# Decay tables read as 2 KB rows, and weight tiles loaded among the first attention loads

## The chip, the cores and the metric

The kernel runs on one core of one Trainium2 chip. The metric is the device time of one execution in microseconds (us). The kernel before took 637.29 us, the median of three runs (636.66 to 637.46).

## What is computed

A decayed linear attention (2 batches, 8 heads, 768 positions, head size 64), whose output is reshaped to 1536 tokens by 512 features, goes through two feed-forward blocks. The reference computes the attention block by block:

```python
Dmask = np.where(rel >= 0, lam[:, None, None] ** rel[None, :, :], 0.0)
lam_pow = lam[:, None, None] ** (pos[None, :, None] + 1)
intra = np.einsum('bhic,bhjc->bhij', qb, kb) * Dmask[None]
intra = np.einsum('bhij,bhjd->bhid', intra, vb)
inter = np.einsum('bhid,bhde->bhie', qb * lam_pow[None], kv_state)
out[:, :, sl] = intra + inter
kb_dec = kb * rev_pow[None]
kv_state = lam_block[...] * kv_state + np.einsum('bhsd,bhse->bhde', kb_dec, vb)
```

Then `h = x @ w_in`, an activation (0 below -1, `(h + 1)**2 / 4` up to 1, `h` above), `x = g @ w_out` with 2048 hidden features; then `(x @ w_a * x @ w_b) @ w_out` with 1536. The weights arrive as float64 bits.

## The kernel before, in words

**Attention.** The 1536 tokens are 12 chunks of 128, six for each batch. `load_chunk` (L122) brings four tiles of a chunk, 256 KB each: qT, kT, kn and vn, issued on SP's queue. For a chunk `att_scores` (L128) makes 8 score products on TensorE into two PSUM banks; `att_mask` (L141) multiplies the keys by the decay (kd, L145, on VectorE for chunk 0, else on GpSimd), the scores by the decay mask (pm, L154, VectorE) and the queries by the powers (qd, L162, GpSimd, for chunk 3 VectorE); `att_state` (L166) makes the new state from kd and vn; `att_out` (L188) adds the two output products and splits the result into the high and low parts of `xy` (L211 ScalarE, L212 VectorE).

**Tables.** The masks come from powers of lam. `powers` (L77) loads lam, raises it on GpSimd (L90), and a zero row is written to a scratch tensor `rows` in DRAM; `store_powers` (L100) writes the powers there; `tables` (L103) reads them back with shifted, overlapping access patterns into `dmask` (512 KB) and `tabq` (256 KB), in runs of 128 floats (512 B). All of these but the zero row's store go through SP's queue.

**Weights.** `load_w` (L227) loads a [128, 512] weight tile of float64 bits (512 KB); `split_w` (L236) turns it into two float32r parts: two operations on ScalarE (L252, L256), four on VectorE (L253, L257, L260, L263), the rounding on ScalarE (L284) and the remainder on GpSimd (L285). Each `split_w` ends with the next `load_w`. Four raw buffers are there.

**Feed-forward.** `h_bank` (L289) and `ab_bank` make the inner products, 12 matmuls of 512 columns each (L273), `y_bank` and `o_bank` the outer ones. The stages run over groups of hidden features and three blocks of 512 tokens. The attention of chunks 4 to 11 is put between the first inner products by `att_step` (L389).

**Order.** SP's and TensorE's instructions stay in the order of the program; VectorE, ScalarE and GpSimd are ordered by a scheduler. Each engine works its own instructions in order. The order around the change stands in L347 to L382: powers, the first loads, `store_powers`, `tables`, more loads, 10 products of zeros (`warm`, L94), the scores of chunks 0 to 2, 4 products of zeros, then the attention of chunks 0 to 3 with one `split_w` after the state of chunk 2 and one at its end; `ahead(4)` (L438) brings the splits to four before the first stage. A tile pool `t2` of 12 buffers holds the temporaries of masks and splits, `acc` of 16 holds the loaded chunks.

## Time and profile before

| | before |
|---|---|
| median of three runs | 637.29 us |
| span of the profiled execution | 635.7 us |
| TensorE matmul busy | 615.7 us (97%) |
| VectorE busy | 380.9 us (60%) |
| ScalarE busy | 247.4 us (39%) |
| GpSimd busy | 253.0 us (40%) |
| mean granted TensorE clock | 0.987 |

The profile covers one execution. Its span, from the first to the last instruction, is 1.6 us below the median of the runs; no other time of that execution is shown. Engines in the rows: PE is TensorE, PEld its weight loads, DVE VectorE, ACT ScalarE, POOL GpSimd, SP SyncE; a q after the name means the engine's queue of instructions that issue DMAs and wait. L145 is line 145 of the kernel. "idle before <-releaser" tells how long an engine stood idle before an instruction and what ended that. PEclk is the granted TensorE clock as a share of full speed.

### The profile page before, as it was taken

The numbers are of one execution on the slowest core, as the hardware profiler recorded it, in microseconds if no ns is written. First come the engines' busy times: TensorE is split into PE (matmuls) and PEld (weight loads), VectorE is DVE, ScalarE is ACT, GpSimd is POOL, SyncE is SP. The second block draws the span as 40 slices with busy tenths as digits, with TensorE's granted clock in tenths as the row PEclk, the third lists the DMA queues.
The fourth block names the chain that finished last, engine by engine and source line by source line (L and its number), as shares of the span: only waits on it lengthen the run. The fifth ranks groups of instructions, "written<-read, shape, count | busy, mean of one in ns | idle before, by whom it ended". The sixth has DMA issues, their size and how long they took to land.

```text
span 635.7 us, 7943 instructions
## 1 busy us (share of the span) xinstructions
PE 615.7 (97%) x3012; PEld 507.3 (80%) x3012; DVE 380.9 (60%) x568; ACT 247.4 (39%) x421; POOL 253.0 (40%) x207
## 2 busy tenths in 40 slices
PE   5898799999999999999999999999999999999998
PEld 2777588888888888888888888888888888888886
DVE  0799794746976797588764433455545555555323
ACT  0245243454543354435643544433333333333110
POOL 2657763433533444354665432222223333333210
PEclk9789799999999999999999999999999999999999
DMA  6968321111210121021102122111111111210013
GB/s 185 379 243 293 111 68 34 66 35 66 100 66 34 66 84 56 34 94 66 67 34 67 67 67 67 66 65 62 56 51 69 64 68 66 67 34 1 1 67 133
DMA packets 20503, 52.70 MB, mean 83 GB/s; under 512 B 2408, under 2 KB 4208, under 8 KB 20464
## 3 DMA queue, kind: packets, MB, share of 16 engines
q1 hardware_dynamic: 20448, 52.18, 23.8%
q8 instruction: 24, 0.39, 0.3%
q14 instruction: 15, 0.12, 0.1%
q10 hardware_dynamic: 16, 0.00, 0.0%
HBM read 49.02 MB, written 3.15 MB: 82 GB/s over the span
## 4 chain that ended last, share of the span: by engine, by line
PE 89%; DVE 4%; DMA 2%; POOL 2%; issue 1%; ACT 1%; SPq 0%; DVEq 0%; POOLq 0%; ACTq 0%
PE ps L273 86%; PE ps L199 1%; PE ps L195 1%; PE ps L174 1%; DMA dmask<-rows 1%; DVE v L263 1%; DVE v L260 1%; DMA lamp<-in_lam 1%; DVE hc L253 1%; DVE v L257 1%; DVE pm L154 0%; DMA rows<-base 0%; POOL qd L162 0%; POOL kd L145 0%; DVE x L212 0%
## 5 line engine op out<-in xcount | busy, mean ns | idle before, releaser
L273 PE MATMUL ps<-y,win 128*128 128x512 f32 x864 | 198.8, 389 | 0.0
L273 PEld LDWEIGHTS ps<-y,win 128*128 128x128 f32 x864 | 162.2, 188 | 33.7
L273 PE MATMUL ps<-x,win 128*128 128x512 f32 x576 | 137.1, 396 | 3.3 <-DVE pm L154 2.6
L273 PE MATMUL ps<-g,wout 128*128 128x512 f32 x576 | 132.6, 389 | 0.0
L273 PEld LDWEIGHTS ps<-x,win 128*128 128x128 f32 x576 | 109.0, 190 | 27.4 <-ACT x L211 2.8
L273 PEld LDWEIGHTS ps<-g,wout 128*128 128x128 f32 x576 | 108.0, 188 | 22.6 <-issue 0.2
L285 POOL TENSOR_TENSOR win<-v,win 128x512 fp32r<-128x512 f32 x40 | 52.2, 1304 | 151.7 <-ACT win L284 151.7
L285 POOL TENSOR_TENSOR g<-r,g 128x512 fp32r<-128x512 f32 x48 | 67.2, 1399 | 85.3 <-ACT g L284 59.8
L273 PE MATMUL ps<-wout,g 128*128 128x512 f32 (+1 forms) x438 | 100.8, 386 | 0.0
L253 DVE TENSOR_SCALAR hc<-hc 128x512 f32<-128x512 f32 x68 | 37.2, 548 | 101.7 <-ACT hc L252 101.4
L273 PEld LDWEIGHTS ps<-wout,g 128*128 128x128 f32 x438 | 81.5, 188 | 16.7
L317 DVE TENSOR_TENSOR acc<-acc,ps 128x512 f32<-128x512 f32 (+1 forms) x97 | 64.7, 678 | 47.2 <-PE ps L273 47.2
L285 POOL TENSOR_TENSOR wout<-v,wout 128x512 fp32r<-128x512 f32 x28 | 36.8, 1313 | 85.1 <-ACT wout L284 85.0
L260 DVE SCALAR_TENSOR_TENSOR v<-raw,v 128x512 int32<-128x512 int32 x68 | 67.4, 991 | 2.3
L293 DVE SCALAR_TENSOR_TENSOR r<-r 128x512 f32<-128x512 f32 x48 | 37.9, 789 | 50.1 <-ACT r L292 50.1
L263 DVE CUSTOM_DVE_ANT_0 v<-v,c 128x1024 uint16<-128x1024 uint16 x68 | 56.3, 828 | 6.0
L284 ACT CAST win<-v 128x512 fp32r<-128x512 f32 x40 | 24.9, 622 | 87.1 <-DVE v L263 87.1
L302 ACT COPY a<-ps 128x512 f32<-128x512 f32 x36 | 21.1, 587 | 95.0 <-PE ps L273 93.6
L285 POOL TENSOR_TENSOR g<-a,g 128x512 fp32r<-128x512 f32 x36 | 46.5, 1292 | 25.8 <-ACT g L284 25.8
L292 ACT ACTIVATE r<-ps,half 128x512 f32<-128x512 f32 x48 | 32.8, 683 | 46.9 <-PE ps L273 46.9
L257 DVE TENSOR_SCALAR v<-hc 128x512 int32<-128x512 int32 x68 | 43.9, 646 | 5.0 <-DVE hc L253 0.9
L252 ACT ACTIVATE hc<-raw 128x512 f32<-128x512 f32 x68 | 45.3, 666 | 0.9 <-DMA raw<-in_w1i 0.9
(46 smaller groups left out, 395.4 us busy)
## 6 DMA issues: line engine op xcount, KB each, us to landing
raw<-in_w2ab SPq DMA_DIRECT2D x24, 512.0 KB, 3.2
raw<-in_w1i SPq DMA_DIRECT2D x16, 512.0 KB, 3.3
raw<-in_w1o SPq DMA_DIRECT2D x16, 512.0 KB, 3.2
raw<-in_w2o SPq DMA_DIRECT2D x12, 512.0 KB, 3.3
qT<-in_att SPq DMA_DIRECT2D x12, 256.0 KB, 4.7
kT<-in_att SPq DMA_DIRECT2D x12, 256.0 KB, 4.5
kn<-in_att SPq DMA_DIRECT2D x12, 256.0 KB, 5.2
vn<-in_att SPq DMA_DIRECT2D x12, 256.0 KB, 5.1
```

The costliest lines, as they stand in the source:

```text
L252: nc.scalar.activation(out=hc.bitcast(F32), in_=high.bitcast(F32), func=ACTF.Abs)
L253: nc.vector.tensor_scalar(out=hc.bitcast(F32), in0=hc.bitcast(F32), scalar1=HIGH_MIN, scalar2=HIGH_MAX, op0=ALU.max, op1=ALU.min)
L257: nc.vector.tensor_scalar(out=v, in0=hc, scalar1=3, scalar2=0x3FFFFFFF, op0=ALU.logical_shift_left, op1=ALU.bitwise_and)
L260: nc.vector.scalar_tensor_tensor(out=v, in0=high, scalar=-0x40000000, in1=v, op0=ALU.bitwise_and, op1=ALU.bitwise_or)
L263: nc.vector.tensor_tensor(out=v, in0=v, in1=c, op=ALU.add)
L273: nc.tensor.matmul(out=ps, lhsT=l[a], rhs=r[b], start=(i == 0 and j == 0), stop=(i == n - 1 and j == 2))
L284: nc.scalar.copy(hi, src)
L285: nc.gpsimd.tensor_tensor(out=lo, in0=src, in1=hi.bitcast(F32), op=ALU.subtract)
L292: nc.scalar.activation(out=r, in_=ps, func=ACTF.Relu, scale=0.5, bias=half)
L293: nc.vector.scalar_tensor_tensor(out=r, in0=r, scalar=1.0, in1=r, op0=ALU.min, op1=ALU.mult)
L302: nc.scalar.copy(a, pa)
L317: nc.vector.tensor_tensor(out=total, in0=total, in1=ps, op=ALU.add)
```

## The change

The scratch tensor `rows` becomes two rows, one for the even and one for the odd heads, with the four heads of one exponent side by side: 128 x 4 zeros, 4 ones, then the powers 1 to 128. lam is read to all partitions, so that the power is one GpSimd operation with no VectorE work on the base before it. The loads and stores of the tables go through ScalarE's queue. A table is read as rows of 512 floats (2 KB), four heads interleaved, and turned to head-major order by one copy each on VectorE, ScalarE and GpSimd. In the written order the four first weight tiles are loaded among the first attention loads, two `split_w` stand ahead of the tables, the others after the states of chunks 1 and 3, the fourth chunk's loads one step earlier, and 8 products of zeros follow the scores of each of the chunks 0 to 2 (24 in place of 4).

```diff
-PITCH = 272
+PITCH = (2 * CH + 1) * H // 2
...
-    lamp = const.tile([128, 1], F32, name="lamp")
-    base = const.tile([128, 8], F32, name="base")
-    exi = const.tile([128, 8], I32, name="exi")
-    exf = const.tile([128, 8], F32, name="exf")
-    zrow = const.tile([H, CH + 1], F32, name="zrow")
-    dmask = const.tile([128, H, CH], F32, name="dmask")
+    lamp = const.tile([128, H], F32, name="lamp")
+    base = const.tile([128, 2, H // 2], F32, name="base")
+    exi = const.tile([128, H], I32, name="exi")
+    exf = const.tile([128, H], F32, name="exf")
+    one = const.tile([2, H // 2], F32, name="one")
+    dmask = const.tile([128, 2, H // 2, CH], F32, name="dmask")
...
-    rows = dram.tile([H, PITCH], F32, name="rows")
+    rows = dram.tile([2, PITCH], F32, name="rows")
...
     def powers():
-        nc.sync.dma_start(out=lamp, in_=bass.AP(tensor=lam.tensor, offset=lam.offset, ap=[[1, H], [0, 16], [1, 1]]))
-        nc.gpsimd.iota(exi, pattern=[[1, 8]], base=0, channel_multiplier=8)
-        nc.vector.memset(base, 0.0)
-        nc.vector.memset(zrow[:, 0:CH], 0.0)
-        nc.vector.memset(zrow[:, CH:CH + 1], 1.0)
+        nc.scalar.dma_start(out=lamp, in_=bass.AP(tensor=lam.tensor, offset=lam.offset, ap=[[0, 128], [1, H]]))
+        nc.gpsimd.iota(exi, pattern=[[0, H]], base=1, channel_multiplier=1)
+        nc.vector.memset(idle, 0.0)
+        zrow = t2("zrow")
+        nc.vector.memset(zrow[0:2], 0.0)
+        nc.vector.memset(one, 1.0)
         nc.vector.memset(half, 0.5)
-        nc.scalar.dma_start(out=rows[:, 0:CH + 1], in_=zrow)
-        nc.vector.tensor_scalar(out=exi, in0=exi, scalar1=127, scalar2=None, op0=ALU.bitwise_and)
         nc.vector.tensor_copy(exf, exi)
-        nc.vector.tensor_scalar(out=exf, in0=exf, scalar1=1.0, scalar2=None, op0=ALU.add)
-        nc.vector.tensor_scalar(out=base, in0=base, scalar1=lamp, scalar2=None, op0=ALU.add)
-        nc.gpsimd.tensor_tensor(out=base, in0=base, in1=exf, op=ALU.pow)
+        nc.scalar.dma_start(out=rows[:, 0:CH * H // 2], in_=zrow[0:2])
+        nc.scalar.dma_start(out=rows[:, CH * H // 2:(CH + 1) * H // 2], in_=one)
+        nc.gpsimd.tensor_tensor(
+            out=base, in0=lamp.rearrange("p (a e) -> p e a", e=2), in1=exf.rearrange("p (a e) -> p e a", e=2),
+            op=ALU.pow,
+        )
+        nc.scalar.dma_start(out=raw_ap((CH + 1) * H // 2, [[H // 2, 128], [PITCH, 2], [1, H // 2]]), in_=base)
...
-    def store_powers():
-        nc.sync.dma_start(out=raw_ap(CH + 1, [[PITCH, H], [8, 16], [1, 8]]), in_=base)
-
     def tables():
-        for i in range(2):
-            nc.sync.dma_start(
-                out=dmask[:, 4 * i:4 * i + 4], in_=raw_ap(1 + 4 * i * PITCH, [[1, 128], [PITCH, H // 2], [1, CH]])
-            )
-        for e in range(2):
-            nc.sync.dma_start(
-                out=tabq[64 * e:64 * e + 64],
-                in_=raw_ap(CH + 1 + e * PITCH, [[0, 64], [2 * PITCH, H // 2], [1, CH]]),
-            )
+        win = [t2("pw") for _ in range(3)]
+        for e in range(2):
+            nc.scalar.dma_start(out=win[e], in_=raw_ap(e * PITCH + H // 2, [[H // 2, 128], [1, 512]]))
+        for e in range(2):
+            nc.scalar.dma_start(
+                out=win[2][64 * e:64 * e + 64], in_=raw_ap(e * PITCH + (CH + 1) * H // 2, [[0, 64], [1, 512]])
+            )
+        turned = [w.rearrange("p (i a) -> p a i", a=H // 2) for w in win]
+        nc.vector.tensor_copy(dmask[:, 0], turned[0])
+        nc.scalar.copy(dmask[:, 1], turned[1])
+        nc.gpsimd.tensor_copy(tabq, turned[2])
...
-                in1=dmask[:, :, CH - 1:CH].rearrange("p (a e) i -> p a e i", e=2).to_broadcast([128, H // 2, 2, D]),
+                in1=dmask[:, :, :, CH - 1:CH].rearrange("p e a i -> p a e i").to_broadcast([128, H // 2, 2, D]),
...
-                in1=dmask.rearrange("p (a e) i -> p e a i", e=2)[:, i], op=ALU.mult,
+                in1=dmask[:, i], op=ALU.mult,
...
         powers()
-        nc.vector.memset(idle, 0.0)
         load_chunk(0, (0, 1))
+        load_w()
+        load_w()
+        load_chunk(0, (2, 3))
         load_chunk(1, (0, 1))
+        load_w()
+        load_chunk(1, (2, 3))
         load_chunk(2, (0, 1))
-        store_powers()
-        load_chunk(0, (2, 3))
-        tables()
-        load_chunk(1, (2, 3))
-        load_chunk(3, (0, 1))
+        load_w()
         load_chunk(2, (2, 3))
-        load_w()
-        load_chunk(3, (2, 3))
-        load_w()
+        load_chunk(3)
         warm(10)
         for c in range(3):
             att_scores(c)
-        warm(4)
+            warm(8)
+        split_w()
+        split_w()
+        tables()
         att_mask(0)
         att_state(0)
         att_mask(1)
         att_out(0)
         att_state(1)
         att_scores(3)
+        split_w()
         att_mask(2)
         att_out(1)
         att_state(2)
-        split_w()
         att_mask(3)
         att_out(2)
+        load_chunk(4)
         att_state(3)
-        load_chunk(4)
+        split_w()
         att_out(3)
-        split_w()
         load_chunk(5)
```

## Rows read from the trace of the kernel before

**Rows 1.** Busy time by stretches: us, busy (instructions) by engine, PEclk, DMA share, GB/s.
```profile
0.00:17.20 17.20, 8.81 (x62) 4.67 (x63) 1.92 (x11) 1.28 (x1) 3.38 (x9) 0.96 0.69 188
17.20:24.00 6.80, 6.78 (x49) 6.00 (x49) 4.13 (x9) 1.82 (x3) 4.02 (x5) 0.61 1.05 395
24.00:37.20 13.20, 11.29 (x107) 9.64 (x105) 12.18 (x20) 3.53 (x6) 10.50 (x12) 0.87 0.77 294
37.20:47.50 10.30, 10.30 (x78) 8.27 (x78) 10.17 (x16) 4.68 (x9) 3.52 (x3) 1.00 0.83 287
47.50:78.40 30.90, 24.98 (x196) 20.14 (x194) 26.81 (x39) 12.02 (x23) 23.71 (x22) 0.89 0.61 210
78.40:160.00 81.60, 80.87 (x442) 67.12 (x442) 54.06 (x73) 39.02 (x69) 33.42 (x26) 1.00 0.16 52
160.00:635.70 475.70, 472.66 (x2091) 391.42 (x2090) 271.62 (x405) 185.05 (x315) 174.51 (x133) 1.00 0.18 61
```

**Rows 2.** The timeline of PE: start us, us, operation, idle before and releaser.
```profile
6.48 1.16 PE L133 MATMUL ps<-qT,kT 64*128 64x128 f32 x16 [0.75 <-DMA kT<-in_att]
...
10.24 1.04 PE L98 MATMUL ps<-idle 128*128 128x512 bf16 x4
17.22 2.05 PE L174 MATMUL ps<-vn,kd 128*128 128x128 f32 x8 [5.94 <-DVE kd L145]
19.20 1.98 PE L199 MATMUL ps<-pm,vn 128*64 128x128 f32 x16
21.11 1.84 PE L174 MATMUL ps<-vn,kd 128*128 128x128 f32 x8
...
25.06 1.09 PE L199 MATMUL ps<-pm,vn 128*64 128x128 f32 x16
26.08 1.16 PE L174 MATMUL ps<-vn,kd 128*128 128x128 f32 x8
...
32.42 1.76 PE L195 MATMUL ps<-qd,st 128*128 128x128 f32 x8 [1.70 <-DVE qd L162]
34.11 1.98 PE L199 MATMUL ps<-pm,vn 128*64 128x128 f32 x16
...
71.42 0.80 PE L273 MATMUL ps<-x,win 128*128 128x512 f32 x1 [2.58 <-DVE pm L154]
```

**Rows 3.** The chain that ended last, 0 to 20 us: start us, us, what.
```profile
0.73 4.04 DMA lamp<-in_lam
...
5.68 1.65 POOL base L90
...
7.35 2.82 DMA rows<-base
...
10.62 5.69 DMA dmask<-rows
```

**Rows 4.** The timeline of DVE: first and last operation of the first split.
```profile
25.76 0.51 DVE L253 TENSOR_SCALAR hc<-hc 128x512 f32<-128x512 f32 x1
...
31.09 0.68 DVE L263 CUSTOM_DVE_ANT_0 v<-v,c 128x1024 uint16<-128x1024 uint16 x1
```

**Rows 5.** Groups of DVE by line, 17 to 80 us: busy us, mean ns.
```profile
L260 DVE SCALAR_TENSOR_TENSOR v<-raw,v 128x512 int32<-128x512 int32 x7 | 7.9, 1135 | 0.2
L257 DVE TENSOR_SCALAR v<-hc 128x512 int32<-128x512 int32 x7 | 6.5, 922 | 0.2
L253 DVE TENSOR_SCALAR hc<-hc 128x512 f32<-128x512 f32 x8 | 5.6, 698 | 0.2
L263 DVE CUSTOM_DVE_ANT_0 v<-v,c 128x1024 uint16<-128x1024 uint16 x7 | 5.4, 777 | 0.2
```

**Rows 6.** Groups by line of ACT and of POOL, 16 to 80 us.
```profile
L211 ACT CAST x<-ps 128x512 fp32r<-128x512 f32 x9 | 5.2, 578 | 26.7 <-PE ps L199 26.6
...
L162 POOL TENSOR_TENSOR qd<-qT,tabq 128x512 f32<-128x512 f32 x7 | 9.1, 1300 | 0.1
```

**Rows 7.** Waits of SP's queue, 0 to 60 us: total us, times, longest.
```profile
SPq L126 <- DMA dmask<-rows: 1.3, 1, 1.3
```

## The prediction

> **What bounds the kernel now.** I read the busy time by stretches first, because an average over the span hides where TensorE loses time. From 160 us to the end PE is busy 472.66 of 475.70 us at full clock, and from 78.4 to 160 us 80.87 of 81.60 [rows 1]. There the change touches nothing, and whatever it wins must be won before 78.4 us: PE then arrives at the saturated part earlier by that much, and the end moves with it.
>
> Before 78.4 us three stretches lose. Up to 17.2 us PE waits for the decay tables. From 17.2 to 37.2 us, the attention of chunks 0 to 3, PE is nearly always busy at first, but at a granted clock of 0.61, a mix of its two levels (1.2 and 2.4 GHz), and then 1.91 us idle (13.20 less 11.29) at 0.87. From 47.5 to 78.4 us it is idle 5.92 us, and the clock is 0.89 [rows 1]. In these stretches VectorE is the fullest engine: 12.18 of 13.20 us, 10.17 of 10.30, 26.81 of 30.90 [rows 1].
>
> The timeline of PE then says who ends the waits: 5.94 us before the first state product, for kd on VectorE; 1.70 us before chunk 3's output, for a qd on VectorE; 2.58 us at 71.42 us, for a mask product on VectorE [rows 2]. The chain of waits traces the first of them back: lam loaded 4.04 us, power 1.65, its store 2.82, the mask read back 5.69 [rows 3]. So the start hangs on a chain of DMAs, and the rest up to 78.4 us on VectorE, which does the weight splits between the masks: the first one's four operations begin at 25.76 us, and the last of them at 31.09 us runs just ahead of the qd that PE waits for [rows 2, 4]. A split there costs VectorE 1.135 + 0.922 + 0.698 + 0.777 = 3.53 us [rows 5]. Meanwhile VectorE works 1.92 us in the first 17.2 us [rows 1].
>
> **The change, part by part. The table chain.** The power no longer waits for VectorE's four small operations between lam's arrival at 4.77 us and 5.68 us; it can start 0.9 us earlier, if lam lands as before. Its store moves to ScalarE's queue and now meets the loads issued by SP. The nearest rows for a small store are 2.82 us, with few loads beside it, and 5.69 us for a read among others [rows 3]; I take 3.7, nearer the first since it moves as few bytes, so the gain of 0.9 is spent. The tables' bytes are the same, 0.79 MB, in 384 pieces of 2 KB where there were 1536 of 512 B. Their time lies between 2.0 us (0.79 MB at the 395 GB/s of the saturated stretch [rows 1]) and a full wait behind SP's loads (the first rival). I take what the read took before, 5.69 us: larger pieces speak for less, loads of 6.29 MB beside it for more. So the mask lands at about 16.3 us, as before. New are the three turning copies. No row has a strided copy; the nearest are a ScalarE cast of 0.58 us and a GpSimd operation of 1.30 us of the same size [rows 6]. I take 0.7 us on the path (VectorE and ScalarE run side by side), bounds 0.6 and 1.3. The copy on GpSimd feeds only qd and the state, which come later; uncovered it would cost 1.3 us. kd then starts near 17.1 us.
>
> **The zeros and the clock.** PE must do the scores of chunk 2 and 8 zeros before the first state product. Up to the end of chunk 2's queries and keys SP's queue now has 4.19 MB: three weight tiles of 0.52 MB, chunks 0 and 1 whole (1.05 MB each) and these 0.52 MB. Chunk 0's tiles (0.52 MB) let the scores start at 6.48 us [rows 2]; without lam ahead of them on SP I take 5.5. The other 3.67 MB at 395 GB/s are 9.3 us, and about 0.6 MB of the tables in between 1.6 us: 16.4 us. Scores of 1.16 us and eight zeros of 1.04 / 4 = 0.26 us [rows 2] give 16.4 + 1.16 + 2.1 = 19.7 us for the first state product, 2.5 us after the 17.22 of before: **2.5 us lost**. The bounds are nothing (kd later than all this) and the late tables below. In return PE comes to it straight from work. Before, after 5.94 us idle, it did state, output, state in 2.05 + 1.98 + 1.84 us; the same groups later take 1.16, 1.09 and 1.16 [rows 2]: **2.5 us won**, or nothing if the zeros don't hold the clock.
>
> **Splits out of the attention.** Two splits, 7.1 us of VectorE, move into a time when it did 1.92 us in 17.2. ScalarE (1.28 us busy) and GpSimd (3.38 us) have room there too [rows 1]. Tiles three and four are loaded early as well, so that their splits can follow in the wait or between the masks; what that gives stands with the late stage. Gone is the 1.70 us wait before chunk 3's output and the slow clock behind it (1.76 + 1.98 against 1.16 + 1.09, 1.5 us) [rows 2]: **3.2 us won**; between 0 and 3.2 if another wait takes the place. Late next is GpSimd: it is busy 4.02 + 10.50 of the 20 us up to 37.2 [rows 1], none of that shrinks, and the turned table comes on top. I take **1 us lost** for it.
>
> **The stage of 47.5 to 78.4 us.** At most PE wins its idle 5.92 us and the clock, 0.11 of 24.98 = 2.7 us: 8.6 us. From 37.2 on VectorE had 10.17 + 26.81 = 37.0 us of work; less the third and fourth split, 7.1, which have moved ahead of it, it has 29.9, against PE's 10.30 + 24.98 - 2.7 = 32.6 [rows 1]. So PE becomes the longer of the two, but GpSimd (27.2 us in the same time) and short chains keep some waits. I take six tenths, **5.3 us won**; bounds 0 and 8.6.
>
> **Edits at no cost.** load_chunk(4) moves past one state product on SP's queue, where later weights already wait for buffers. The 16 zeros after chunks 0 and 1 run while PE would wait for data; without that wait they would cost 16 x 0.26 = 4.2 us. The masks' new layout leaves the operations' sizes alone; if they turned slow, 24 of them would each cost VectorE something, so I look at them.
>
> **Sum:** -2.5 + 2.5 + 3.2 - 1.0 + 5.3 = 7.5 us. The profiled span is 635.7 us, 1.6 us below the median of 637.29, which I take as what lies around it: 628.2 + 1.6 = **629.8 us**.
>
> **The rivals. First, the tables come late, and the gain is small.** The transfers share engines that the loads saturate: the DMA share is 1.05 at 395 GB/s as soon as weights and chunks are queued together [rows 1]. If the reads got through only behind all loads, 6.29 + 0.79 MB at 395 GB/s from about 4 us end at 22 us; with copy and kd the first state product is at 23.4 us, 6.2 us late. Of the terms above 2.5 + 3.2 - 1.0 + 5.3 = 10.0 us remain: 3.8 us faster, 633.5 us; down to 636 if the later stage gives nothing more. For it: the wait of SP's queue for an older transfer's landing, 1.3 us [rows 7], shows that new transfers are held back by earlier ones. Against it: the reads are issued from another queue. The Trainium skill ("DMA: Bandwidth & Descriptors", section "Issuing engines are not separate DMA queues") speaks against the move: DMAs issued by different engines run on the same 16 engines and interleave, and only issue time is saved. By its section on queues, rings and completion order, an engine takes turns between the queues that have work; an equal share would read the tables in an estimated 4.0 us. No row here shows two busy queues.
>
> **Second, PE is packed.** All of the late stage's loss goes, and the start loses nothing: 0 + 2.5 + 3.2 + 8.6 = 14.3 us, 623.0 us. For it: VectorE's sum falls below PE's. Against: the waits on GpSimd.
>
> **Third, no net change,** 636 to 638.5 us: VectorE's relief is real, but GpSimd's masks and remainders end the same waits. GpSimd's 23.71 of 30.90 us [rows 1] is a weak argument for it; the releasers shown are mostly VectorE [rows 2].
>
> **Fourth, slower:** ScalarE's queue holds the reads. It works in order, and in the changed kernel it has the split's three operations as well as the table's DMAs; if the scheduler puts the reads behind the roundings of all four splits, they wait for the fourth tile. That is loaded to 4.72 MB, about 16 us; its split follows at about 21.5 us, and the mask lands 5.69 us later at 27.2. The state starts at 28.7 us, 11.5 us late; the idle PE loses the clock again (0 for 2.5); 3.2 - 1.0 + 5.3 us remain: 4.0 us slower, 641.3 us. It decides from a first state product later than 17.22 + 10.0 = 27.2 us. Against it: in the written order only two splits stand ahead of the tables.
>
> **How the numbers follow.** A measurement of this kernel can tell about 0.2% (1.3 us) from no change. Forecast (5 to 11 us won) 0.52; late tables (1.3 to 5 us won) 0.17; packed 0.10; no change 0.09; slower 0.12. Faster is 0.52 + 0.17 + 0.10 = 0.79. The range from 624.0 to 637.3 us leaves out the slower case, half of the packed one and a little of no change, some 0.19.
>
> **What would show it.** Right: the first state product between 18 and 21 us, at full clock; two or more splits by VectorE before 17 us; no wait before chunk 3's output; idle PE from there to the saturated part halved. Wrong: the state product after 23 us (table chain; look at the issue of the reads on ScalarE's queue), PE waits that end with GpSimd, a mask or copy operation above 1.3 us, or zeros with a slow clock behind them.

## The result, and the profile after

The changed kernel takes 642.53 us (median of 6 runs, 639.99 to 643.88) against 637.02 for the kernel before in the same comparison: ratio 1.0089, 95% interval 1.0065 to 1.0113. It is slower by 0.9%; the forecast was 629.8 us, the range ended at 637.3. In the table below medians decide; the times of single stages come from one profiled execution each, and such executions lie up to some 2.5 us off the median of their runs. The changed kernel's was the slowest of its six, 643.88 us.

The busy time by stretches of the changed kernel answers to [rows 1]:

```profile
0.00:17.20 17.20, 12.54 (x73) 6.30 (x74) 6.58 (x13) 4.82 (x7) 4.84 (x10) 0.90 0.85 279
17.20:24.00 6.80, 3.03 (x16) 1.73 (x14) 3.16 (x4) 2.36 (x4) 4.00 (x4) 0.87 0.79 256
24.00:37.20 13.20, 12.36 (x110) 10.68 (x108) 12.92 (x22) 3.42 (x6) 9.98 (x10) 0.81 0.72 242
37.20:47.50 10.30, 8.47 (x58) 6.58 (x60) 5.42 (x9) 1.43 (x3) 7.48 (x7) 0.83 0.78 267
47.50:78.40 30.90, 26.03 (x236) 21.26 (x232) 27.27 (x39) 11.92 (x21) 15.27 (x14) 1.00 0.64 219
78.40:160.00 81.60, 79.34 (x431) 66.21 (x432) 54.47 (x72) 36.88 (x63) 38.00 (x32) 0.98 0.16 52
160.00:642.00 482.00, 479.01 (x2119) 396.68 (x2118) 274.21 (x409) 188.38 (x320) 175.50 (x134) 1.00 0.18 61
```

VectorE did its early splits (6.58 us of work ahead of 17.2 us where it did 1.92), but TensorE, the first number behind each stretch's length, is busy for only 3.03 of the 6.80 us from 17.2 to 24 us. From 37.2 to 47.5 us VectorE, made lighter, is busy 5.42 of 10.30 us, and TensorE loses there too.

The chain of waits of the changed kernel, which answers to [rows 3] (start, us, what):

```profile
1.64 5.67 DMA raw<-in_w1i
...
7.33 0.68 ACT hc L255
...
8.46 0.09 DVE exf L86
...
8.63 1.82 POOL base L89
...
10.47 5.18 DMA rows<-base
...
17.31 3.02 DMA pw<-rows
...
20.33 1.10 ACT dmask L114
...
21.45 0.04 DVE kd L148
```

The power starts at 8.63 us (before 5.68). It does not wait for lam but for a small cast of the exponents on VectorE (L86), which the scheduler put behind the first operation of the first split, and that waits for the first weight tile. The store takes 5.18 us (2.82) and ScalarE's turning copy 1.10 us. The 3.02 us of the reads count from ScalarE's last issue; the second mask window, for which that copy waits, was issued at 16.07 us and took 4.2 us (5.69).

TensorE's timeline of the changed kernel, which answers to [rows 2]; the last row is the first product with the second weights, behind which TensorE is packed:

```profile
23.02 2.05 PE L177 MATMUL ps<-vn,kd 128*128 128x128 f32 x8 [3.77 <-issue]
25.00 1.98 PE L202 MATMUL ps<-pm,vn 128*64 128x128 f32 x16
26.91 2.08 PE L177 MATMUL ps<-vn,kd 128*128 128x128 f32 x8
...
39.32 1.16 PE L136 MATMUL ps<-qT,kT 64*128 64x128 f32 x16
...
42.05 0.50 PE L276 MATMUL ps<-x,win 128*128 128x512 f32 x1 [1.57 <-ACT x L214]
42.78 4.36 PE L276 MATMUL ps<-x,win 128*128 128x512 f32 x11 [0.22 <-DVE x L215]
47.07 1.16 PE L136 MATMUL ps<-qT,kT 64*128 64x128 f32 x16
...
71.14 1.16 PE L198 MATMUL ps<-qd,st 128*128 128x128 f32 x8 [2.49 <-POOL qd L165]
...
77.42 0.49 PE L276 MATMUL ps<-x,win 128*128 128x512 f32 x1 [1.91 <-ACT x L214]
...
93.30 1.50 PE L177 MATMUL ps<-vn,kd 128*128 128x128 f32 x8 [2.26 <-POOL kd L148]
94.45 4.36 PE L276 MATMUL ps<-x,win 128*128 128x512 f32 x12
...
105.52 11.18 PE L276 MATMUL ps<-g,wout 128*128 128x512 f32 x48
```

Three marks of the same timeline of the kernel before, to compare with:

```profile
36.02 1.24 PE L133 MATMUL ps<-qT,kT 64*128 64x128 f32 x16
...
40.22 1.16 PE L133 MATMUL ps<-qT,kT 64*128 64x128 f32 x16
...
99.17 11.18 PE L273 MATMUL ps<-g,wout 128*128 128x512 f32 x48
```

So the lag changes in three steps. First state product: 23.02 against 17.22, 5.80 us late. Scores of chunk 4 (the end of the first attention): 39.32 against 36.02, so 2.50 us came back. First product with the second weights: 105.52 against 99.17, so 3.05 us were lost again. That loss lies at the stage's start: the scores of chunk 5 come at 47.07 against 40.22, already 6.85 us late. Sum: 6.35 us late, and the spans differ by 642.1 - 635.7 = 6.4 us.

### The profile page after: what moved, and what is told of

Read it like the earlier page. It is cut to its first block, busy times and chain, and to the rows that moved or that the text cites. A ratio compares the mean times of both kernels' runs of the same rounds, so it can differ in the third digit from the quotient of the medians.

```text
span 642.1 us, 7983 instructions
## 1 busy us (share of the span) xinstructions
PE 620.8 (97%) x3031; PEld 509.5 (79%) x3032; DVE 384.0 (60%) x565; ACT 249.2 (39%) x422; POOL 255.1 (40%) x208
## 4 chain that ended last, share of the span: by engine, by line
PE 88%; DVE 6%; DMA 2%; issue 1%; ACT 1%; POOL 1%; ACTq 0%; SPq 0%; DVEq 0%; POOLq 0%
PE ps L276 86%; DVE pm L157 1%; DMA raw<-in_w1i 1%; DVE hc L256 1%; DMA rows<-base 1%; DVE x L215 1%; PE ps L202 1%; DVE st L189 1%; DVE v L266 1%; PE ps L198 1%; PE ps L177 1%; DVE r L296 1%; DMA pw<-rows 0%; DVE r L297 0%; PE ps L136 0%
## 5 line engine op out<-in xcount | busy, mean ns | idle before, releaser
L256 DVE TENSOR_SCALAR hc<-hc 128x512 f32<-128x512 f32 x68 | 40.7, 599 | 108.2 <-ACT hc L255 108.1
L288 POOL TENSOR_TENSOR g<-a,g 128x512 fp32r<-128x512 f32 x36 | 46.5, 1291 | 25.8 <-ACT g L287 25.8
L259 ACT ACTIVATE c<-raw 128x512 int32<-128x512 uint32 x68 | 45.1, 664 | 3.0 <-POOL base L89 1.7
```

The costliest lines, as they stand in the source:

```text
L256: nc.vector.tensor_scalar(out=hc.bitcast(F32), in0=hc.bitcast(F32), scalar1=HIGH_MIN, scalar2=HIGH_MAX, op0=ALU.max, op1=ALU.min)
L259: nc.scalar.activation(out=c, in_=low.bitcast(U32), func=ACTF.Copy, scale=2.0**-29)
L288: nc.gpsimd.tensor_tensor(out=lo, in0=src, in1=hi.bitcast(F32), op=ALU.subtract)
```

## The experiments

All were timed beside the kernel before on the same chip. Each ratio is to the kernel before in that run's own comparison, where its median lay between 635.7 and 637.0 us. "Table chain" runs from the issue of the powers' store to the landing of the last mask window (the second read for `dmask`); "1st state", "scores 4" and "packed" are the marks at the first state product, the scores of chunk 4 and the first product with the second weights. The edits are shown in part.

| kernel | median us | ratio [95%] | power's store issued | table chain | 1st state | scores 4 | packed |
|---|---|---|---|---|---|---|---|
| before | 637.0 | 1 | 7.35 | 9.0 | 17.22 | 36.02 | 99.17 |
| changed | 642.5 | 1.0089 [1.0065, 1.0113] | 10.47 | 9.9 | 23.02 | 39.32 | 105.52 |
| e1 cast on GpSimd | 641.6 | 1.0083 [1.0062, 1.0103] | 8.79 | 14.0 | 25.12 | 40.33 | 103.28 |
| e2 tables only | 640.0 | 1.0056 [1.0038, 1.0075] | 6.88 | 12.9 | 21.67 | 37.71 | 100.79 |
| e3 weights only | 641.5 | 1.0071 [1.0049, 1.0093] | 11.01 | 8.1 | 20.01 | 39.20 | 100.64 |
| e4 4 zeros | 639.8 | 1.0060 [1.0038, 1.0081] | 10.43 | 9.4 | 22.54 | 37.34 | 100.53 |
| e5 tables on SP | 634.8 | 0.9981 [0.9965, 0.9996] | 6.90 | 8.2 | 16.99 | 32.98 | 96.34 |
| e6 SP, one tile early | 640.9 | 1.0068 [1.0042, 1.0094] | 6.76 | 9.7 | 19.36 | 38.78 | 102.81 |
| e7 SP held | 642.6 | 1.0099 [1.0068, 1.0130] | 8.53 | 11.3 | 28.77 | 42.16 | 104.85 |
| e8 order by hand | 639.9 | 1.0060 [1.0040, 1.0080] | 6.62 | 13.7 | 22.29 | 37.62 | 100.44 |
| e9 before, free splits | 632.4 | 0.9938 [0.9918, 0.9958] | 7.31 | 8.7 | 16.87 | 31.29 | 93.46 |
| e14 changed, free splits | 642.1 | 1.0084 [1.0069, 1.0098] | 8.41 | 13.2 | 23.54 | 42.38 | 103.66 |
| e10 e5, one tile early | 634.9 | 0.9972 [0.9959, 0.9986] | 6.87 | 8.0 | 16.80 | 34.06 | 95.79 |
| e11 e5, zeros | 635.1 | 0.9976 [0.9959, 0.9993] | 6.95 | 9.1 | 18.01 | 35.88 | 99.23 |
| e12 e5, read in steps | 640.7 | 1.0068 [1.0046, 1.0090] | 6.94 | 8.0 | 15.74 | 35.92 | 104.72 |
| e13 e5, end powers | 634.6 | 0.9976 [0.9960, 0.9991] | 6.83 | 7.5 | 15.34 | 31.22 | 95.90 |
| e15 e5 again | 635.7 | 0.9979 [0.9965, 0.9994] | 6.92 | 8.1 | 17.74 | 32.86 | 96.04 |

### Which half of the change costs: e1 to e4

**e1**, the cast off VectorE's queue:

```diff
-        nc.vector.tensor_copy(exf, exi)
+        nc.gpsimd.tensor_copy(exf, exi)
```

> The changed kernel with one edit: the cast of the exponents (L86) runs on GpSimd, so that it no longer stands in VectorE's queue behind the first operation of the first weight split. Theory A (the start is late because the power waited for that cast): the power starts near 5 us in place of 8.63, its store is issued before 9.5 us in place of 10.47 (ScalarE still has three split operations ahead of it), the first state product starts 1 to 3.5 us earlier than 23.0 us, and the time falls by 1 to 3.5 us against the changed kernel. Rival B (the table's DMAs are slow under the loads of weights and chunks, whenever they are issued): the store lands no earlier than 14.5 us, the first state product stays within 1 us of 23.0, time unchanged within 1 us.

Theory A falls; B holds, but for the state product, which comes 2.1 us later where B left it within 1 us. The power starts at 5.14 us, but its store, issued at 8.79 behind ScalarE's split operations, takes 6.99 us and the second mask window 6.50. The cast's place keeps the power back by 3.5 us in the changed kernel, but it is not what the time hangs on.

**e2**, the new tables on ScalarE's queue, with the order of loads, splits and zeros of the kernel before (here against that kernel):

```diff
         load_chunk(2, (0, 1))
-        store_powers()
         load_chunk(0, (2, 3))
```

> The changed kernel's tables (new layout, 2 KB reads, turning copies, ScalarE's queue) with the order of loads, splits and zeros of the kernel before: no weight is loaded or split ahead of the attention. Theory A (the early weights, by queue order and by traffic, make the start late; the tables' new form by itself is harmless): the first state product starts at 17.2 us or up to 2 us before, and the time is that of the kernel before within 1.5 us or up to 2 us below. Rival B (the new form of the tables is what costs): the first state product later than 19 us and at least 2 us slower than the kernel before.

No weight is loaded early and no split stands early, and 0.56% is lost all the same. The store is issued early, at 6.88 us, but the table chain takes 12.9 us in place of 9.0. So the tables' part of the change makes a loss by itself; e5 below tells the layout from the queue.

**e3**, the other half: the tables of the kernel before, with the weights loaded and split ahead:

```diff
         load_chunk(0, (0, 1))
+        load_w()
+        load_w()
         load_chunk(1, (0, 1))
...
         warm(4)
+        split_w()
+        split_w()
```

> The kernel before with its own tables (SP's queue, 512 B pieces), but with two weight tiles loaded ahead of them and two splits written ahead of the attention. The small VectorE operations for the power again stand behind the first split's first operation. Theory A: the power waits for the first weight tile's arrival (7 to 8.5 us in place of 5.68), the first state product starts 2 to 5 us later than 17.2, and the time is 0 to 5 us above the kernel before. Rival (only the new tables are at fault): the first state product within 1 us of 17.2 and at least 3 us faster than the kernel before, for the splits done in the wait.

Here the chain stays short (8.1 us; the store takes 2.34), but VectorE's exponent steps stand behind the first split, and the store is issued 3.7 us late. The state product is 2.8 us late, as theory A had it; the time, 5.2 us up, lies just above its range. Each half thus makes a loss of its own: one by a late start of the chain, the other by a long chain.

**e4**, 4 products of zeros in place of 24:

```diff
-            warm(8)
+        warm(4)
```

> The changed kernel with the products of zeros of the kernel before: 4 after the scores of chunk 2 in place of 8 after each of the chunks 0 to 2. Theory A (PE waits for kd anyway, the zeros cost nothing and, ending at 19.3 us, do not hold the clock until 23.0): time within 1 us of the changed kernel, the state, output and state products after the wait take about 2.0 us each as before. Rival (the zeros are in the way of the scores): 1 to 3 us faster than the changed kernel.

2.8 us below the changed kernel by the medians, the rival's size, though the two intervals overlap. It changes more than the zeros: the scheduler wrote another order for VectorE and GpSimd. What it shows for certain is that the zeros kept no clock in the changed kernel: the first state product takes 2.05 us with them and without.

### Why the table chain is long: e5 to e8

**e5**, the new layout and its 2 KB reads, but store and reads on SP's queue at their old places, in the old order; the cast on GpSimd:

```diff
-            nc.scalar.dma_start(out=win[e], in_=raw_ap(...))
+            nc.sync.dma_start(out=win[e], in_=raw_ap(...))
```

> The changed kernel's table layout, 2 KB reads and turning copies, with the powers' store and the tables' reads back on SP's queue, and the order of loads, splits and zeros of the kernel before (the exponents' cast on GpSimd). Only lam and the two constant rows stay on ScalarE's queue. Theory C (SP waiting for the powers, and then for their store, kept the loads away, so that store and reads went through quickly; on ScalarE's queue they run beside a full stream of loads): the store lands within 3.2 us of its issue, the mask's two reads within 5 us of theirs, and the first state product starts at 16 to 18.5 us (21.67 with the same order on ScalarE's queue); time within 2 us of the kernel before. Rival D (the new layout and its copies are what costs): first state product later than 19 us, 2 us or more slower than the kernel before.

**Faster than both kernels**, than the one before by 0.2%. The layout, the large reads and the copies do no harm; the move of the store and the reads to the other queue does. The DMA view from 5 to 24 us in 40 slices of 0.475 us shows it as GB/s. First the kernel before:

```profile
GB/s 380 401 414 401 410 405 401 61 47 22 39 254 401 319 79 82 126 271 342 344 184 200 166 215 205 263 401 380 392 379 388 397 388 427 401 384 392 401 414 414
```

Then e5:

```profile
GB/s 401 401 414 410 414 375 48 69 13 60 168 164 375 306 129 103 220 345 323 216 190 190 311 298 380 401 388 414 410 431 423 418 388 384 384 418 405 401 440 388
```

Then e8, told of below, whose tables go by ScalarE's queue:

```profile
GB/s 444 405 414 423 414 384 405 388 410 392 378 389 427 379 354 354 397 375 401 457 410 384 367 388 401 392 375 392 298 207 229 336 229 306 306 336 401 431 405 418
```

In the first two there is a hole of 13 to 69 GB/s at 8 to 10 us, and a thin stretch behind 12 us. They are there because SP, waiting first for the power and then for its store, issues only one pair of tiles meanwhile. The store lands in the first hole (3.19 us in e5), the reads follow in thin traffic. On ScalarE's queue SP goes on issuing, the DMA engines never fall below 350 GB/s before 18 us, and the same 4 KB store takes about 6 us. The waits of SP's queue that looked like a cost [rows 7] belong to the short chain. Whether it is the hole that lets the store through is asked again in e10.

**e6**, the changed order on SP's queue with one tile loaded and split ahead, the order up to the tables written out for all engines:

```diff
-        load_w()
-        load_chunk(0, (2, 3))
         load_chunk(1, (0, 1))
-        load_w()
-        load_chunk(1, (2, 3))
+        store_powers()
+        load_chunk(0, (2, 3))
```

> As the run before, and one weight tile loaded and split ahead: SP's queue holds chunk 0's queries and keys, weight tile 0, chunk 1's queries and keys, the powers' store, then two more pairs of tiles, the tables' reads and all other loads; the order up to the tables is written out for all engines, so that the power stands ahead of the split everywhere. Theory C: the store lands within 4 us of its issue, first state product at 16.5 to 19 us with one split done before 13 us; time 0 to 4 us below the kernel before. Rival D: first state product after 19.5 us, slower than the kernel before by 2 us or more.

Theory C's store, but neither theory's start, and 5.2 us slower than the kernel before. The store landed in 3.2 us again, but the reads were issued behind two more chunk pairs and took 6.1 to 6.4 us. TensorE waited for GpSimd's kd and qd (4.4 and 2.9 us) and for kT (3.8 us). A quick store is thus not enough; the reads must be quick too.

**e7**, the changed kernel with the cast on GpSimd and SP held by a 16-byte read of the stored powers:

```diff
+        load_chunk(1, (0, 1))
+        nc.sync.dma_start(out=gate, in_=raw_ap((2 * CH) * H // 2, [[1, 1], [1, 4]]))
         load_chunk(0, (2, 3))
-        load_chunk(1, (0, 1))
```

> The changed kernel with the exponents' cast on GpSimd, its table DMAs still on ScalarE's queue, but SP's queue held: after chunk 0's queries and keys, two weight tiles and chunk 1's queries and keys, a 16-byte DMA on SP reads a part of the stored powers, so that all later loads wait for the store. Theory C (traffic, not the queue, is what delays the store): issued near 9 us, it lands within 3.5 us (6.99 us with the loads beside it), the reads start before 13 us, and the first state product starts before 20 us, 3 us or more ahead of the 25.12 us without the hold. Rival E (ScalarE's queue is slow by itself): the store takes 5 us or more and the first state product stays after 22 us.

Theory C holds for the store, not for the start (28.77 us; C had it before 20). Against e1 the hold is new, and chunk 1's queries and keys stand ahead of chunk 0's other pair. Issued at 8.53 us on the same ScalarE queue, the store lands within 2.65 us, where e1 took 6.99. ScalarE's queue, then, is not slow by itself; what SP issues beside it counts. As a kernel it is worse, since the held loads come late: TensorE waits 11.07 us for chunk 2's kT.

**e8**, the changed kernel with the first instructions of all engines in an order written by hand: cast, power and store ahead of the splits:

```diff
-    with tc.manual_schedule(engines={SP, PE}):
+    with tc.manual_schedule(engines={SP, PE, DVE, Activation, Pool}):
```

> The changed kernel with the order written out for all engines up to the second split: the exponents' cast, the power and its store stand ahead of the splits on VectorE, GpSimd and ScalarE; loads and queues as in the changed kernel. Theory A (the order on the engines is what delays the tables): the store is issued before 7.5 us, lands before 11 us, first state product before 19.5 us, 3 us or more faster than the changed kernel. Theory C (the stream of loads delays the store, whenever it is issued): issued before 7.5 us it still lands after 12 us, first state product at 20 us or later, within 2.5 us of the changed kernel's time.

Theory C again. The store is issued at 6.62 us, 3.9 us earlier than in the changed kernel, and the state product comes only 0.7 us earlier: the store takes 6 us and the last mask window 7.17 us. The time is 2.7 us below the changed kernel's; the first products ran at full rate here (told below).

### What the splits were worth: e9 and e14

**e9**, the kernel before; for the first two weight tiles it leaves out two operations on ScalarE and four on VectorE each, so it computes something else:

```diff
+        if nxt["split"] <= 2:
+            v = high
+        else:
             hc = ...
```

> The kernel before, with the first two weight tiles split for almost nothing: their two ScalarE passes and four VectorE passes are left out (the two tiles are then taken as the upper halves of the bits, so that part of the computation is another one), the loads and the order of the rest stay. It is the upper bound of what taking two splits out of the attention can bring, with no price paid ahead of it. Theory L (the prediction's steps: a wait of 1.7 us before chunk 3's output, the slow clock behind it, and 6 tenths of VectorE's freed time in 47 to 78 us): 3 us or more faster, below 634 us, and the first product of a gate group with the second weights starts 3 us or more earlier than 99.2 us. Rival M (that time of VectorE was not what TensorE waited for; its waits there are a chain chunk output, ScalarE x, VectorE x, first product of the block): within 1.2 us of the kernel before.

Theory L by the time: 3.9 us faster by the medians. But the timeline says where:

```profile
16.87 1.74 PE L174 MATMUL ps<-vn,kd 128*128 128x128 f32 x8 [4.63 <-DVE kd L145]
...
29.27 1.06 PE L195 MATMUL ps<-qd,st 128*128 128x128 f32 x8
30.26 1.10 PE L199 MATMUL ps<-pm,vn 128*64 128x128 f32 x16
31.29 1.16 PE L133 MATMUL ps<-qT,kT 64*128 64x128 f32 x16
...
93.46 11.20 PE L276 MATMUL ps<-g,wout 128*128 128x512 f32 x48
```

The wait before chunk 3's output and the slow products behind it (32.42 and 34.11 in [rows 2]) are gone. From first state product to scores of chunk 4 are 14.42 us in place of 18.80, 4.4 us won. From there to the packed part it is 62.17 in place of 63.15, only 1.0 us. The two splits left out are those that stand at 25.8 to 38.7 us of the kernel before, so e9 measures them and not the third and fourth.

**e14**, the same edit on the changed kernel.

> The changed kernel, with its first two weight tiles split for almost nothing (two ScalarE and four VectorE passes of each left out, so that this part of the computation is another one), as was done to the kernel before, where it brought 3.9 us. Theory F (the move has taken the two splits off the path; the loss is all in the tables and what waits for them): 641 to 643 us, within 1.2 us of the changed kernel, and the first product of a gate group with the second weights stays at 104.5 to 105.5 us. Rival G (the splits still cost, now ahead of the tables, by holding the exponents, the copy or ScalarE's queue): 3 us or more below the changed kernel, under 639.5 us.

Theory F by the time: nothing is won. By stages it is not so clean, since the rest of the order moved too. The store is issued 2.1 us earlier and the table chain is 13.2 us long; the first attention takes 18.84 us (42.38 - 23.54) in place of 16.30, with a wait of 3.41 us for a state on VectorE; from the scores of chunk 4 to the packed part it is 61.28 in place of 66.20. That the two splits are off the path in the changed kernel, as the change wanted, is likely and not shown. e2, without early splits, does its first attention in 37.71 - 21.67 = 16.0 us, the changed kernel in 39.32 - 23.02 = 16.3: the early splits brought nothing there that e2 lacks.

### Towards a better version: e10 to e13, and e15

**e10** puts one weight tile ahead of the store in e5 and splits it behind the scores (against e5):

```diff
         load_chunk(2, (0, 1))
+        load_w()
         store_powers()
...
         warm(4)
+        split_w()
         att_mask(0)
```

> The faster variant (new layout of the tables, store and reads on SP's queue) with one weight tile loaded ahead of the store of the powers and split right behind the scores, in place of the first split inside the attention. If the early split is worth its share (theory L): 1 to 2 us faster than that variant's 634.8 us. If it is worth nothing (M) and the tile only fills the lull in which the store landed (3.2 us there): the store takes 4 us or more, the first state product comes 1 to 2 us later than 17.0 us, and the time is 0.5 to 2 us above that variant's.

Neither: the store stays at 3.30 us and the start keeps its time, but nothing that can be measured is won over e5. The tile does fill the hole, as the DMA view from 5 to 24 us shows:

```profile
GB/s 401 410 397 405 405 436 427 423 320 391 401 259 26 103 177 229 384 328 173 211 194 267 310 392 349 336 332 397 392 384 397 405 410 418 414 414 414 392 388 388
```

From 6.87 to 10.17 us, while the store is under way, the engines move 320 to 436 GB/s, and it takes about as long as in a hole (3.19 us in e5, 3.31 in e12). So neither a high rate alone (e10) nor ScalarE's queue alone (e7) makes the store slow; it is slow on ScalarE's queue while SP goes on issuing loads. Why is not shown.

**e11** gives e5 more zeros:

```diff
-        warm(4)
+        warm(20)
```

> The same faster variant with 20 products of zeros behind the scores in place of 4, at 0.26 us each ending at about 16.3 us, beside the first state product at 17.0 us. Theory Z (the first products behind a wait of 4.9 us run at half rate because TensorE stood still, and zeros up to them cure it): the first state products of chunk 0 take 1.2 us in place of 2.0 and its output products 1.1 in place of 1.8, and the time is 0.5 to 1.6 us below that variant's 634.8 us, as far as the next wait (a first product held to 36.4 us by VectorE's x) does not take it. Rival: zeros end later than the keys are ready and hold the state product, or the rate stays low: no gain, up to 1 us loss.

Not shown to help. The first state product runs at full rate (1.13 us), but the next two groups take 1.95 and 1.99. The stretches of e11 (the first number after the length is TensorE's busy time, then in the order of [rows 1]):

```profile
15.60:18.00 2.40, 0.00 (x0) 0.02 (x1) 0.78 (x2) 1.09 (x1) 0.76 (x1) 1.00 1.03 316
18.00:19.00 1.00, 0.99 (x8) 0.95 (x8) 1.00 (x2) 0.00 (x0) 1.00 (x2) 1.00 1.05 385
19.00:23.00 4.00, 4.00 (x28) 3.46 (x28) 2.94 (x6) 1.05 (x2) 3.85 (x5) 0.57 1.06 401
23.00:27.00 4.00, 4.00 (x48) 3.59 (x49) 3.85 (x6) 1.36 (x3) 3.85 (x5) 1.00 1.02 392
```

TensorE stands still for 2.4 us at a granted clock of 1.00, does its first products still at 1.00, and is granted 0.57 (mostly the lower level of 1.2 GHz) while it is packed. The slow time comes behind the pause.

**e12** reads the mask windows of e5 in place, in steps of four numbers, without the copies.

```diff
-        nc.vector.tensor_copy(dmask[:, 0], turned[0])
-        nc.scalar.copy(dmask[:, 1], turned[1])
...
-                in1=dmask[:, i], op=ALU.mult,
+                in1=dmask[:, i].rearrange("p i a -> p a i"), op=ALU.mult,
```

> The faster variant (new layout, 2 KB reads, all on SP's queue) with the two mask windows read where they lie, in steps of four numbers, instead of turned by a copy first: the copies on VectorE (0.62 us) and ScalarE (1.09 us) go, and the keys with decay wait only for the reads. Theory T (those copies stand on the path to the first state product): the keys with decay start at about 15.0 us in place of 16.2, the first state product at about 15.8 in place of 17.0, and if that is kept to the end the time is about 633.6, 1.2 us below that variant's 634.8 and 0.4 per cent below the kernel before. Rival: reading in steps slows the mask products (0.68 us in the copied layout) or the gain is eaten by the next wait; then the time is 634.8 or above.

Theory T holds up to the first state product (15.74) and not beyond. The mask products of e12 on VectorE, 15 to 160 us:

```profile
L156 DVE TENSOR_TENSOR pm<-ps,dmask 128x512 f32<-128x512 f32 x24 | 25.3, 1086 | 0.2
```

and those of e5:

```profile
L159 DVE TENSOR_TENSOR pm<-ps,dmask 128x512 f32<-128x512 f32 x24 | 15.4, 684 | 0.2
```

Read in steps each takes 0.4 us more, VectorE has 9.9 us more to do there, and the kernel is 0.7% slower than the one before where e5 is 0.2% faster. The turning copies pay.

**e13** keeps them and copies the end powers apart, so that the keys with decay wait for the reads alone; **e15** repeats e5 beside it.

```diff
+        for e in range(2):
+            nc.vector.tensor_copy(kend[:, e], win[e][:, 508:512])
```

> The faster variant with the turned copies kept for the mask products (in steps they took 1.08 us in place of 0.68), and only the eight end powers of each window copied by themselves, so that the keys with decay wait for the reads and not for ScalarE's copy. Theory T (what was gained ahead of the first state product is kept as long as the mask products stay at 0.68): keys with decay at about 15.3 us in place of 16.2, first state product at about 16.1 in place of 17.0, time 0.5 to 1 us below that variant's on the same chip. Rival: the first outputs wait for the masks anyway, or VectorE's queue takes the gain back: same as that variant within 0.4 us.

> The faster variant once more, unchanged, on the same chip as the others of this call: 634 to 636 us, 0.1 to 0.4 per cent below the kernel before. If it comes out at the time of the kernel before, the variant is no faster and only the same.

e5's gain is there a second time (0.9979), about the 0.2% that a measurement can tell. e13's median is 1.0 us below e15's, its ratio (0.9976) the same within the intervals. e13 starts the state product 2.4 us before e15 and reaches chunk 4's scores 1.6 us earlier, yet the packed part comes at 95.90 against 96.04. Part of the gain is given back here:

```profile
67.25 0.50 PE L281 MATMUL ps<-x,win 128*128 128x512 f32 x1 [2.58 <-ACT x L219]
68.81 5.06 PE L281 MATMUL ps<-x,win 128*128 128x512 f32 x11 [1.06 <-DVE x L220]
```

At the first product of the next block TensorE waits for the chunk's output, ScalarE's x and VectorE's x in turn: a chain, not a full engine. e15 waits there nearly as long (2.29 and 1.07 us), so it is only a part: e13 leads by 4.3 us at the scores of chunk 5 (36.17 against 40.48), by 1.7 us at the 11 products (68.81 against 70.48), and these take it 5.06 us where e15 needs 4.24.

## Why the prediction was wrong

By the marks the start gave -5.80 us where the sum had -2.5, the first attention +2.50 where it had +4.7 (2.5 + 3.2 - 1.0), and the late stage -3.05 where it had +5.3.

**The table chain, "the mask lands at about 16.3 us, as before": this step failed.** The keys with decay started at 21.45 us where they had started at 16.43. The power was late by 3.1 us (store issued 10.47 against 7.35), because the cast at L86 was taken to follow lam and in truth followed a split on VectorE. Chain and copy were 0.9 and 1.1 us longer, and kd itself 0.8 us (1.47 against 0.70): 5.9 us, against the 5.8 that the state product was late. The store, taken as 3.7 us "nearer the first since it moves as few bytes", took 5.18, and about 6 to 7 in e1, e2 and e8: its bytes were the wrong guide, the loads that SP goes on issuing beside ScalarE's queue the right one (e7, e10). The reads gained from a stall in turn: SP's queue stood 6.5 us waiting for one of them, and the second mask window took 4.2 us in place of 5.69. With the power in time and the loads flowing it took 6.5 and 7.2 us (e1, e8). That is why mending the power alone saves little.

**The zeros and the clock, -2.5 and +2.5.** The zeros didn't set the start; the tables did. The sum for the zeros held (they ended at 19.25 us, the estimate was 19.7), but TensorE then stood still until 23.02, and the 2.5 us won did not come: the three groups took 2.05, 1.98 and 2.08 us, as in [rows 2]. Where the state product followed sooner the mechanism is there. In e8 it comes 1.23 us behind the zeros:

```profile
22.29 1.13 PE L177 MATMUL ps<-vn,kd 128*128 128x128 f32 x8 [1.23 <-DVE kd L148]
23.35 1.14 PE L202 MATMUL ps<-pm,vn 128*64 128x128 f32 x16
```

The third group takes 1.16 us, and e14's three 1.13, 1.18 and 1.16. This term fell with the late tables, not by itself.

**Splits out of the attention, +3.2 - 1.0.** Right as a mechanism: e9 wins 4.4 us there. But 2.5 us is all that came back, and e2 had as much without the change's splits, so they are not shown to have brought it.

**The late stage, +5.3 (six tenths of 8.6 are 5.2): this step failed too, and by the most.** VectorE's sum of work was not the limit: from 37.2 to 78.4 us it came to 32.7 us (5.42 + 27.27; the prediction had 29.9), less than TensorE's 34.5 (8.47 + 26.03). From the scores of chunk 4 to those of chunk 5 the changed kernel takes 47.07 - 39.32 = 7.75 us, the one before 40.22 - 36.02 = 4.20; from there to the second weights 58.45 against 58.95. So all of the loss lies in the first 7.75 us. VectorE has little to do then (5.42 us from 37.2 to 47.5), but TensorE waits 1.57 us for ScalarE's x and then needs 4.36 us for 11 products, at a lower clock, that take 2.79 us at 78.38. Chunk 3's output products end at 39.39 us; ScalarE comes to x two microseconds later, behind the rounding of the fourth split, for which it waits on VectorE:

```profile
40.90 0.62 ACT L287 CAST win<-v 128x512 fp32r<-128x512 f32 x1 [4.28 <-DVE v L266]
41.42 0.58 ACT L214 CAST x<-ps 128x512 fp32r<-128x512 f32 x1
```

The change put that split ahead of chunk 3's output in the written order. No run moved it alone, so its price stays open; in e14, where the rounding comes before those output products end (39.97 against 42.44), the stage takes 61.28 us, 1.9 less than in the kernel before, the most that any run of the changed order shows of the 5.3. From 47 us to the packed part the relief of VectorE is real, and other engines take its place: TensorE's waits for VectorE fall from 3.7 to 0.5 us, those for GpSimd rise from 3.0 to 4.8 and those for ScalarE from nothing to 1.9. The GpSimd waits stay with free splits (2.48 and 2.27 us in e14) and shrink to 1.55 and 0.59 in e4, where the scheduler wrote another order. That the order is their cause is likely; no run changed it alone, so it stays open.

**The rivals.** The first, late tables, had the mechanism and the mark (after 23 us: 23.02). It had the sign wrong, because it kept the 10.0 us of the other terms. The third, other engines ending the same waits, describes the late stage. The first one's reason, reads behind all loads, was only half of it: the store suffered as much. The Trainium skill's rule named there ("DMA: Bandwidth & Descriptors", "Issuing engines are not separate DMA queues") spoke against the change, and the trace agrees: another queue saved no time on the DMA engines (the table chain took 12.9 us in e2, 9.0 before). The equal share between queues that the prediction took from the Trainium skill, an estimated 4.0 us for the reads, is not what the loaded runs show: in e8 the mask windows alone, two thirds of the bytes, took 7.6 us from the first issue (12.69) to the last landing (20.3). The fourth rival, slower at 641.3 us, came near the time by luck, by a mechanism that was not there: the state product came at 23.02, not 28.7.

## What to carry to other kernels

Before a small transfer is moved to another queue, look at what its old queue will issue once it no longer waits for it: the wait may be what holds the other loads back, and freeing the queue can make the transfer slower (here a store of 2.3 to 3.3 us became one of 5.0 to 7.0). An engine's sum of work in a stage bounds what relief can bring but doesn't promise it; leaving the work out altogether, in one run, measures it, here 3.9 us for two splits, if the work left out is the work that the term counts. When operations are put ahead of others, check on each in-order engine which small operation of the critical chain now stands behind them: here the cast of the exponents on VectorE, and x on ScalarE.

## What the hardware showed that was not expected

- A 4 KB store took 2.3 to 3.3 us on SP's queue, even beside loads at 320 to 436 GB/s (e3, e5; e10), and 2.65 on ScalarE's queue while SP's was held (e7). On ScalarE's queue, while SP went on issuing loads at some 400 GB/s, it took 5.0 to 7.0 us (the changed kernel, e1, e2, e8, e14).
- ScalarE's turning copy of 128 x 512 took 1.09 to 1.11 us, VectorE's 0.61 to 0.63, GpSimd's 1.08 to 1.68; ScalarE's cast of the same size out of PSUM takes 0.58 [rows 6].
- The granted clock can read full while products run at half rate. In e4, with the state product at 22.54 us taking 2.05 us and the output product at 24.51 taking 1.98, the two stretches read 1.00:

```profile
20.00:24.00 4.00, 1.47 (x7) 1.50 (x8) 3.02 (x4) 2.06 (x3) 3.21 (x3) 1.00 0.90 303
24.00:28.00 4.00, 4.00 (x27) 3.41 (x26) 3.87 (x8) 0.58 (x1) 2.78 (x4) 1.00 0.86 323
```

In the changed kernel the same groups stand in a stretch of 0.50 (24 to 28 us). The duration of a product, not the column, tells its rate.
